# A scan and a top-2 mixture of adapters on one core: a new search in the tail, a rank for every operation, and A loaded in 512 B rows

## The chip, the core and the metric

The kernel runs on one core of a Trainium2 chip. The metric is the time of one execution in device microseconds (us). The core has five engines that work side by side: TensorE (PE in the profile, PEld for its weight loads), VectorE (DVE), ScalarE (ACT), GpSimd (POOL) and SyncE (SP), which here only issues transfers. Sixteen DMA engines move the data between the chip's memory (HBM) and the on-chip memory (SBUF). Matmul results land in eight banks of PSUM.

## The reference

First a linear recurrence over 6400 steps, in each of 8 batches and 128 channels; its 51,200 rows of 128 are then the tokens `x` of a mixture of 8 adapters of rank 16, of which each token uses the two with the largest logits.

```python
for t in range(S):                       # a, b: [8, 6400, 128] float32
    h = a[:, t] * h + b[:, t]
    out[:, t] = h
x = out.reshape(51200, 128)
logits = x @ w_gate                      # w_gate [128, 8]
topk = the two largest logits of each row
w = softmax over those two
delta[row] = sum over the two: w * ((x[row] @ A[e]) @ B[e])   # A [8,128,16], B [8,16,128]
return x + delta
```

## The kernel before

The tokens are cut into 100 chunks of 512 (`C`), a chunk into 4 blocks of 128 (`J`). What follows names the operations as the program does; a number behind the name is the chunk (`sc99`), the unit or the gate group.

**Loads.** `la` and `lb` bring two chunks of a and b at a time, 512 KB each, into one of 6 slots of `a_tm` and `b_tm` (`load`, L546, issued by SP). The first four chunks come singly. In most pairs ("paired" chunks) a row of SBUF takes 8 consecutive tokens, 4 KB; chunks 4 to 11 are "flat", with 2 KB per row. The constants come over ACT's queue (L471): A as `[d, e, r]`, pieces of 64 B, then w_gate, then B. `ch` (DVE, L489) casts all three to fp16 in `cst_h`.

**Front, by chunk.** PE transposes a and b into channel-major PSUM tiles pA and pB (`A`, `B`, or `P` for a mixed pair of halves; L567). ACT copies pA to `a_st` (`ae`, L585). DVE's scan `sc` (L618) reads `a_st` and pB and writes x in fp16, channel-major, to `xT` (24 slots); it starts from the last column of the scan before, so the scans follow one another in order.

**Logits, by unit.** A unit is 6 blocks (4 in the first three and the last four units, so that the last four units are chunks 96 to 99). `Z` (PE, L638) multiplies a block of x by `[A | w_gate]`, 136 columns, into pZ; `ze` (ACT, L644) copies the unit to `zl`.

**Gates, by group.** A group is 4 units; the first two groups have 1 and 2 units, the last five (17 to 21) have 2, 1, 1, 1 and 1. For each row of 8 logits the function `gating` finds the two largest and their weights: `g1` first maximum (DVE, L672), `2` logits minus it (L674), `3` -1e30 where that is at least 0 (L676), `5` added, which masks the maximum (L679), `g4` second maximum (DVE, L681), `6` minus it (L683), `7` the two differences added (L685), `w1` sigmoid (ACT, L687), `g8` times "is one of the two" (DVE, L693), which gives `g`. Operations 2, 3, 5, 6 and 7 run on GpSimd (then named `q2` to `q7`), but on DVE in the last six groups (`WIDE_DVE`, 16 to 21).

**Back, by chunk.** `mu` multiplies z by g into `zw` (GpSimd, L712; for the last ten chunks on DVE, as `md`, L716, by the list `MU_DVE`). `T` transposes zw on PE (L725); `te` copies the result to `zwT` (DVE, L734, for some chunks ACT, L731). `D` (PE) adds x, by a product with the identity (L739), and delta, zwT times B (L740), in pO; the last 12 chunks use the banks of pA and pB too. `oe` (ACT, L749) copies the block to `outt`, and SP stores two chunks at a time (L784, 512 KB), the last four chunks singly (256 KB).

One store goes out in parts: `SPLIT = {68: [93, 32, 3]}` cuts the store of chunks 68 and 69 by rows of SBUF into three transfers, of 93, 32 and 3 of its 128 rows.

**The order** on every engine is not written out by hand: `Program.schedule` plans it before the kernel is built. Every operation has a rank, and each engine's operations are sorted by it:

```python
rank[op.i] = op.base + (TEMPLATE[op.kind][op.k] ...) + NUDGE.get(op.name, 0.0)
```

`base` is the chunk's place, `TEMPLATE` an offset for each kind and place in a period of 6 chunks, and `NUDGE` an offset for single operations, nearly all of them in chunks 0 to 17 and from 78 on. Among the operations within `WINDOW[engine]` of the smallest rank the planner takes the one that can start first by its own cost estimates. `waits` then derives the semaphore waits.

Of the kernel before, what the change touches and what calls it, by code (L numbers as in the profile page):

```python
# [10 lines left out]
PERIOD = 6  # L11
# [7 lines left out]
Q_RATE = {3: 3.6e-3, 5: 2.1e-3, 7: 2.1e-3}  # L19
# [87 lines left out]
EARLY = -400  # L107
LEAD = [1, 2]
TAPER = [2, 1, 1, 1, 1]
WIDE_DVE = [1, 2, 3, 4, 5, 6]  # L110
TE_LAST = [1, 2, 4, 6, 8, 10]
TAIL_UNITS = [4, 4, 4, 4]
HEAD_UNITS = [4, 4, 4]
# [47 lines left out]
    "q7": [1.073],  # L161
    "q8": [35.473],
    "g7": [-1.33],
    "g8": [-0.424],
}


# [721 lines left out]
```

## Time and profile before

| | before |
|---|---|
| time, median of 3 runs (lowest to highest) | 203.87 us (203.84 to 204.08) |
| profiled execution, its own time | 204.1 us |
| its span in the profile | 202.2 us |
| mean granted clock of TensorE | 0.995 |
| bytes read from HBM, written | 52.56 MB, 26.21 MB |
| DMA packets under 512 B | 3702 of 30999 |

The span runs from the first to the last record of the profiled execution; the execution's own time also has what lies around it. A line of the form `L618 DVE TENSOR_TENSOR_SCAN xT<-a_st,xT,pB 128x512 ... x96` is a group of instructions: line of the kernel, engine, operation, what it writes and reads, its shape and how many there are. A row of the timeline begins with the start and the duration in us; in brackets stands how long the engine was idle before and what ended it. "issue" is time in which the engine waited for nothing that the profile shows. The busy time of a DVE row includes what of it overlaps its neighbours, so the step from one start to the next is the better price of a short instruction.

### The profile page before, as it was taken

How to read it: one execution, taken by the hardware profiler on the slowest of the kernel's cores; microseconds unless marked ns; L12 is line 12 of the kernel's file. 1: busy time of each engine (PE TensorE's matmuls, PEld its weight loads, DVE VectorE, ACT ScalarE, POOL GpSimd, SP SyncE). 2: the span in 40 equal slices, each digit the busy share in tenths (PEclk: the TensorE clock that was granted, in tenths of full speed). 3: DMA queues.
4: the chain of work that ended last, by engine and by line, in shares of the span. 5: the costliest groups of instructions: out<-in, count | busy, mean ns of one | idle time of the engine just before them, and what ended most of it. 6: DMA issues, size and time to landing. Idle time of an engine off the chain costs nothing.

```text
span 202.2 us, 7464 instructions
## 1 busy us (share of the span) xinstructions
PE 181.5 (90%) x3120; PEld 157.6 (78%) x3120; DVE 176.2 (87%) x291; ACT 172.7 (85%) x314; POOL 139.1 (69%) x176
## 2 busy tenths in 40 slices
PE   6978899999999999999999998987898997989971
PEld 6678777888888888888888887876787886877751
DVE  0679799999999999999999999986898997999970
ACT  2448799999998999999999998987797988978792
POOL 1016559998788898888888889796878997462000
PEclk9999999999999999999999999999999999999998
DMA  6999999999999999999999999999999999999984
GB/s 193 371 390 391 407 410 408 399 413 406 406 412 415 407 410 409 420 410 406 410 414 406 410 410 415 409 411 414 409 411 412 411 416 410 401 377 385 356 331 177
DMA packets 30999, 79.26 MB, mean 392 GB/s; under 512 B 3702, under 2 KB 3830, under 8 KB 30966
## 3 DMA queue, kind: packets, MB, share of 16 engines
q1 hardware_dynamic: 29494, 78.39, 98.6%
q10 hardware_dynamic: 1472, 0.40, 0.9%
q8 instruction: 25, 0.41, 0.8%
q14 instruction: 8, 0.07, 0.1%
HBM read 52.56 MB, written 26.21 MB: 390 GB/s over the span
## 4 chain that ended last, share of the span: by engine, by line
PE 35%; DVE 21%; DMA 14%; ACT 4%; issue 2%; POOL 1%; SPq 0%; DVEq 0%
DVE xT L618 11%; PE pA L567 7%; DMA b_tm<-in_b_dram 7%; PE pZ L638 7%; DMA a_tm<-in_a_dram 6%; PE pB L567 5%; PE pO L725 5%; PE pO L739 5%; PE pO L740 4%; DVE zwT L734 4%; DVE zw L716 3%; ACT outt L749 1%; ACT zl L644 1%; DVE g L693 1%; ACT a_st L585 1%
## 5 line engine op out<-in xcount | busy, mean ns | idle before, releaser
L618 DVE TENSOR_TENSOR_SCAN xT<-a_st,xT,pB 128x512 f16<-128x512 f32 x96 | 120.3, 1253 | 10.3 <-PE pB L567 6.3
L712 POOL TENSOR_TENSOR zw<-zl,g 128x512 f16<-128x512 f32 x90 | 94.3, 1064 | 16.8 <-DVE g L693 11.7
L567 PE MATMUL pA<-ident_f,a_tm 64*128 64x64 f32 (+1 forms) x752 | 68.4, 232 | 4.9 <-DMA b_tm<-in_b_dram 3.1
L567 PE MATMUL pB<-ident_f,b_tm 64*128 64x64 f32 (+1 forms) x752 | 68.7, 232 | 1.9 <-DMA a_tm<-in_a_dram 0.9
L585 ACT COPY a_st<-pA 128x512 f32<-128x512 f32 x100 | 59.8, 606 | 11.4 <-PE pA L567 6.6
L567 PEld LDWEIGHTS pA<-ident_f,a_tm 64*128 64x128 f32 (+1 forms) x752 | 55.5, 139 | 10.8 <-DMA b_tm<-in_b_dram 3.6
L567 PEld LDWEIGHTS pB<-ident_f,b_tm 64*128 64x128 f32 (+1 forms) x752 | 55.4, 139 | 6.9 <-DMA a_tm<-in_a_dram 1.2
L644 ACT COPY zl<-pZ 128x816 f32<-128x816 f32 (+1 forms) x69 | 57.6, 834 | 2.9 <-PE pZ L638 2.7
L749 ACT COPY outt<-pO 128x512 f32<-128x512 f32 x92 | 54.7, 606 | 3.3 <-PE pO L740 2.4
L739 PE MATMUL pO<-ident_h,xT 128*128 128x128 f16 x368 | 50.9, 221 | 2.1 <-ACT zwT L731 1.2
L740 PE MATMUL pO<-cst_h,zwT 128*128 128x128 f16 x368 | 50.1, 219 | 0.0
L739 PEld LDWEIGHTS pO<-ident_h,xT 128*128 128x128 f16 x368 | 40.6, 113 | 3.8 <-ACT zwT L731 1.7
L638 PE MATMUL pZ<-cst_h,xT 128*128 128x136 f16 x400 | 36.1, 225 | 3.4 <-DVE xT L618 2.3
L740 PEld LDWEIGHTS pO<-cst_h,zwT 128*128 128x128 f16 x368 | 36.5, 99 | 0.8 <-issue 0.8
L725 PE MATMUL pO<-ident_h,zw 128*128 128x128 f16 x368 | 35.1, 220 | 1.1 <-POOL k L685 0.4
L638 PEld LDWEIGHTS pZ<-cst_h,xT 128*128 128x128 f16 x400 | 26.4, 115 | 8.4 <-DVE xT L618 5.2
L734 DVE COPY zwT<-pO 128x512 f16<-128x512 f16 x76 | 30.7, 407 | 0.7 <-PE pO L725 0.6
L725 PEld LDWEIGHTS pO<-ident_h,zw 128*128 128x128 f16 x368 | 22.5, 97 | 4.8 <-issue 1.0
L674 POOL TENSOR_TENSOR k<-zl,m 128x192 f32<-128x192 f32 (+2 forms) x16 | 7.9, 493 | 14.1 <-DVE m L672 14.0
L683 POOL TENSOR_TENSOR L<-k,m 128x192 f32<-128x192 f32 (+2 forms) x16 | 7.8, 490 | 9.3 <-DVE m L681 9.3
L676 POOL TENSOR_SCALAR L<-k 128x192 f32<-128x192 f32 (+2 forms) x16 | 12.8, 801 | 1.4
L731 ACT COPY zwT<-pO 128x512 f16<-128x512 f16 x16 | 9.6, 597 | 3.3 <-PE pO L725 3.3
(43 smaller groups left out, 104.7 us busy)
## 6 DMA issues: line engine op xcount, KB each, us to landing
a_tm<-in_a_dram SPq DMA_DIRECT2D x48, 512.0 KB, 13.2
b_tm<-in_b_dram SPq DMA_DIRECT2D x48, 512.0 KB, 13.3
out_dram<-outt SPq DMA_DIRECT2D x47, 512.0 KB, 13.2
a_tm<-in_a_dram SPq DMA_DIRECT2D x4, 256.0 KB, 4.5
out_dram<-outt SPq DMA_DIRECT2D x4, 256.0 KB, 3.3
b_tm<-in_b_dram SPq DMA_DIRECT2D x3, 256.0 KB, 5.5
out_dram<-outt SPq DMA_DIRECT2D x1, 372.0 KB
b_tm<-in_b_dram ACTq DMA_DIRECT2D x1, 256.0 KB, 3.3
```

The lines of the kernel that those rows point to most:

```text
L567: last = eng["pe"].transpose(*args)
L585: lambda: eng["act"].copy(a_st[c % NA][:, :], pA[:, c % 2, :]), fr(c, "ae"))
L618: last = eng["dve"].tensor_tensor_scan(out=x[:, s0:s1], data0=a_st[c % NA][:, s0:s1], data1=pB[:, c % 2, s0:s1], initial=init, op0=ALU.mul ...
L638: last = eng["pe"].matmul(pZ[:, k // (n // 2), o : o + W], xblock(b0 + k), Awg_h)
L644: return eng["act"].copy(zl[:, zb : zb + n, :].rearrange("p (h k) w -> p h (k w)", h=2), pZ[:, :, 0 : n // 2 * W])
L676: lambda e: e.tensor_scalar(out=ll, in0=kk, scalar1=0.0, scalar2=-1.0e30, op0=ALU.is_ge, op1=ALU.mult), dve=not main)
L712: lambda: eng["pool"].tensor_tensor(out=wv, in0=zv, in1=gv, op=ALU.mult), ba(gi, c, "mu"))
L725: last = eng["pe"].transpose(ptile[:, k * 128 : k * 128 + 128], zw[w][:, k, :], ident_h[:, :])
L734: lambda: eng["dve"].tensor_copy(zwT[w][:, :], ptile[:, 0:C]), ba(gi, c, "te"))
L739: eng["pe"].matmul(dst, xblock(b0 + k), ident_h[:, :], start=True, stop=False)
L740: last = eng["pe"].matmul(dst, zwT[w][:, k * 128 : k * 128 + 128], B_h, start=False, stop=True)
L749: lambda: eng["act"].copy(outt[:, o0 : o0 + n, :].rearrange("p k w -> p (k w)"), bank),
```

## The change

It has five parts.

1. **A in 512 B rows.** A is loaded as `araw`, 128 rows of 512 B: row (e, h) holds 8 of the 128 channels (`l`) by 16 ranks (`r`) of expert e. As this is not the layout `cst_h` needs, it is rearranged on chip: two small reductions of the identity on DVE give `own` and `pick`, GpSimd multiplies `araw` by `own` (`cr`, 128x1024, into `spread`), PE sums 8 products with shifted views of `pick` into pZ (`cm`), and ACT copies the sum to `cst_h` (`cc`). Every `Z` depends on `cc` now. `ch` casts w_gate and B alone and is ranked earlier.

2. **A rank per operation.** `TEMPLATE` and `WINDOW` are all zero, and `NUDGE` names a rank for every operation, so that each engine runs its operations in the order of these ranks. The lists of who does what are by chunk now: `te` on ACT in 1, 7, 13, and so on each 6 up to 73, then 78, 80, 82, 83, 84, 89, 91, 92, 94, 96, 97 and 98 (before: the same up to 73, then 79, 85, 90, 92, 94, 96, 98 and 99); `mu` on DVE in 82, 84, 86 and 90 to 99 (before: 90 to 99).

3. **max8 in small groups.** In groups of at most 4 blocks (`TOP8`; groups 0 and 18 to 21) DVE's `max`, which gives the 8 largest of a row in order, runs once per block into `v8`. Operations 2 and 6 subtract its first and second column; 3, 5 and the second reduction fall away.

4. **Gates on GpSimd.** `GATE_DVE` names the gate operations that stay on DVE; all others of 2, 3, 5, 6 and 7 run on GpSimd, in the last groups too. In group 19 (chunk 97) this puts 2, 6 and 7 on GpSimd, in group 20 (chunk 98) 2 and 6, in group 21 (chunk 99) none.

5. **Two output copies on DVE, and the split.** `oe` of chunks 95 and 97 moves from ACT to DVE (`od`). The store of chunks 68 and 69 goes out as 124 and 4 rows.

Besides, one cost estimate for GpSimd's operation 3 and one for `w1` are other numbers, `paired` is renamed `woven`, and there is code for halved chunks and filler transposes that empty lists (`HALF`, `FILL`) leave out.

```diff
 NUDGE = {
-    "A0": -7.373, "A1": 6.112, "A10": -1.64, ...
+    "A0": 404.647, "A1": 403.572, "A10": 13.623, ...       # every operation has one
-WINDOW = {'pe': 42.345, 'act': 35.431, 'dve': 24.751, 'pool': 5.955, 'sp': 63.924}
+WINDOW = {'pe': 0.0, ...}
-WIDE_DVE = [1, 2, 3, 4, 5, 6]
-TE_LAST = [1, 2, 4, 6, 8, 10]
+GATE_DVE = ['2_14', '2_17', '2_18', '2_21', '3_14', '3_16', '5_17', '6_21',
+            '7_16', '7_17', '7_18', '7_20', '7_21']
-TE_ACT = [1]
-MU_DVE = [1, 2, 3, 4, 5, 6, 7, 8, 9, 10]
+TE_ACT = [1, 7, 13, 19, 25, 31, 37, 43, 49, 55, 61, 67, 73, 78, 80, 82, 83, 84, 89, 91, 92, 94, 96, 97, 98]
+MU_DVE = [82, 84, 86, 90, 91, 92, 93, 94, 95, 96, 97, 98, 99]
+OE_DVE = [95, 97]
-SPLIT = {68: [93, 32, 3]}
+SPLIT = {68: [124, 4]}
+TOP8 = 4
 ...
-            ("ca", 0.94, cst_f[:, 0:128].rearrange("p (e r) -> p e r", e=E),
-             moe_A.rearrange("e d r -> d e r")),
+            ("ca", 0.3, araw[:, :], moe_A.rearrange("e (h l) r -> (e h) (l r)", l=DL)),
 ...
+        o_cr = P.add(
+            "pool", "cr", 2.1, [(o_c[0], True), (o_own, True)],
+            lambda: eng["pool"].tensor_tensor(
+                out=spread[:, :, :].rearrange("q l (e r) -> q l e r", e=E),
+                in0=araw[:, :].rearrange("q (l r) -> q l r", l=DL).unsqueeze(2).broadcast_to([128, DL, E, R]),
+                in1=own[:, :].unsqueeze(1).unsqueeze(3).broadcast_to([128, DL, E, R]),
+                op=ALU.mult),
+            START,
+        )
+        def gather():
+            for k in range(DL):
+                last = eng["pe"].matmul(
+                    pZ[:, 0, 0:128], pick[:, DL - 1 - k : DL - 1 - k + 128], spread[:, k, :],
+                    start=k == 0, stop=k == DL - 1)
+            return last
+        o_cc = P.add("act", "cc", 0.3, [(o_cm, True)],
+                     lambda: eng["act"].copy(cst_h[:, 0:128], pZ[:, 0, 0:128]), (EARLY, "cc", 0))
 ...
+            top = nb <= TOP8
+            def maxes():
+                for k in range(nb):
+                    last = eng["dve"].max(out=t8[:, k, :], in_=Lp[:, k, :])
+                return last
+            if top:
+                b1, b2 = (t8[:, :, k : k + 1].to_broadcast([128, nb, E]) for k in (0, 1))
+                d2 = wide(2, ..., lambda e: e.tensor_tensor(out=kk, in0=Lp, in1=b1, op=ALU.subtract))
+                d5 = wide(6, ..., lambda e: e.tensor_tensor(out=ll, in0=Lp, in1=b2, op=ALU.subtract))
+            else:
+                d2, d5 = search()        # 2, 3, 5, g4, 6 as before
 ...
+            if c in OE_DVE:
+                o_oe[c] = P.add("dve", f"od{c}", ..., lambda: eng["dve"].tensor_copy(ov, bv), ...)
+            else:
+                o_oe[c] = P.add("act", f"oe{c}", ..., lambda: eng["act"].copy(ov, bv), ...)
```

More of the change, by code (lines that the diff above doesn't have):

```diff
@@ new lines @@
+    "la": [0.0, 0.0, 0.0],
+    "lb": [0.0, 0.0, 0.0],
+    "A": [0.0, 0.0, 0.0, 0.0, 0.0, 0.0],
+    "B": [0.0, 0.0, 0.0, 0.0, 0.0, 0.0],
+    "ae": [0.0, 0.0, 0.0, 0.0, 0.0, 0.0],
+    "sc": [0.0, 0.0, 0.0, 0.0, 0.0, 0.0],
+    "Z": [0.0, 0.0, 0.0, 0.0],
+    "ze": [0.0, 0.0, 0.0, 0.0],
+    "g1": [0.0],
+    "g2": [0.0],
+    "g3": [0.0],
+    "g4": [0.0],
+    "g5": [0.0],
+    "g6": [0.0],
+    "w1": [0.0],
+    "w2": [0.0],
+    "p1": [0.0],
+    "p2": [0.0],
+    "p3": [0.0],
+    "mu": [0.0, 0.0, 0.0, 0.0, 0.0, 0.0],
@@ new lines @@
+    "T": [0.0, 0.0, 0.0, 0.0, 0.0, 0.0],
+    "te": [0.0, 0.0, 0.0, 0.0, 0.0, 0.0],
+    "D": [0.0, 0.0, 0.0, 0.0, 0.0, 0.0],
+    "oe": [0.0, 0.0, 0.0, 0.0, 0.0, 0.0],
+    "st": [0.0, 0.0, 0.0],
+    "ta": [0.0, 0.0, 0.0, 0.0, 0.0, 0.0],
+    "md": [0.0, 0.0, 0.0, 0.0, 0.0, 0.0],
+    "wu": [0.0],
+    "fi": [0.0, 0.0, 0.0, 0.0, 0.0, 0.0],
+    "ch": [0.0],
+    "cm": [0.0],
+    "cc": [0.0],
+    "mb": [0.0],
+    "q2": [0.0],
+    "q3": [0.0],
+    "q5": [0.0],
+    "q6": [0.0],
+    "q7": [0.0],
@@ L588, in front @@
             r0 = rows[c]
-            if not paired(c):
+            o_fi = []
+            for k in range(FILL.get(c, 0)):
+                o_fi.append((P.add(
+                    "pe", f"fi{c}_{k}", 0.109, [(o_id, True)] + get(o_sc, c - 2),
+                    lambda: eng["pe"].transpose(pB[:, c % 2, 0:128], ident_f[:, :], ident_f[:, :]), fr(c, "fi")), True))
+            if not woven(c):
                 o_A[c] = P.add("pe", f"A{c}", 0.109 * J, deps_a(c), trans(part_a(c)), fr(c, "A"))
-                o_B[c] = P.add("pe", f"B{c}", 0.109 * J, deps_b(c), trans(part_b(c)), fr(c, "B"))
+                o_B[c] = P.add("pe", f"B{c}", 0.109 * J, deps_b(c) + o_fi, trans(part_b(c)), fr(c, "B"))
                 add_ae(c)
@@ L669, in wide @@
                              lambda: f(eng["pool"]), ga(gi, f"q{kind}"))
-            d1 = P.add("dve", f"g1_{gi}", 0.142 + nb * E * 1.04e-3, [(o_ze[u], True) for u in range(u0, u0 + n)] + old,
-                       lambda: eng["dve"].tensor_reduce(out=v1, in_=Lp, axis=X, op=ALU.max), ga(gi, "g1"))
-            d2 = wide(2, [(d1, True)] + old,
-                      lambda e: e.tensor_tensor(out=kk, in0=Lp, in1=bc(v1), op=ALU.subtract), dve=not main)
-            d3 = wide(3, [(d2, True)],
-                      lambda e: e.tensor_scalar(
-                          out=ll, in0=kk, scalar1=0.0, scalar2=-1.0e30, op0=ALU.is_ge, op1=ALU.mult), dve=not main)
@@ L686, in gating, with search @@
-            a1 = P.add("act", f"w1_{gi}", 0.15 + nb * E * 0.86e-3, [(d6, True)] + old,
+            top = nb <= TOP8
+            t8 = v8[s][:, 0:nb, :] if top else None
+            def search():
+                d2 = wide(2, [(d1, True)] + old,
+                          lambda e: e.tensor_tensor(out=kk, in0=Lp, in1=bc(v1), op=ALU.subtract))
+                d3 = wide(3, [(d2, True)],
+                          lambda e: e.tensor_scalar(
+                              out=ll, in0=kk, scalar1=0.0, scalar2=-1.0e30, op0=ALU.is_ge, op1=ALU.mult))
+                d3 = wide(5, [(d3, True)],
+                          lambda e: e.tensor_tensor(out=ll, in0=ll, in1=kk, op=ALU.add))
+                d4 = P.add("dve", f"g4_{gi}", 0.142 + nb * E * 1.04e-3, [(d3, True)],
+                           lambda: eng["dve"].tensor_reduce(out=v2, in_=ll, axis=X, op=ALU.max), ga(gi, "g4"))
+                d5 = wide(6, [(d4, True)],
+                          lambda e: e.tensor_tensor(out=ll, in0=kk, in1=bc(v2), op=ALU.subtract))
+                return d2, d5
@@ new lines, in maxes, with first @@
+            def maxes():
+                for k in range(nb):
+                    last = eng["dve"].max(out=t8[:, k, :], in_=Lp[:, k, :])
+                return last
+            def first():
+                return eng["dve"].tensor_reduce(out=v1, in_=Lp, axis=X, op=ALU.max)
+            d1 = P.add("dve", f"g1_{gi}", 0.09 + 0.075 * nb if top else 0.142 + nb * E * 1.04e-3,
+                       [(o_ze[u], True) for u in range(u0, u0 + n)] + old, maxes if top else first, ga(gi, "g1"))
+            if top:
+                b1, b2 = (t8[:, :, k : k + 1].to_broadcast([128, nb, E]) for k in (0, 1))
+                d2 = wide(2, [(d1, True)] + old,
+                          lambda e: e.tensor_tensor(out=kk, in0=Lp, in1=b1, op=ALU.subtract))
+                d5 = wide(6, [(d1, True)] + old,
+                          lambda e: e.tensor_tensor(out=ll, in0=Lp, in1=b2, op=ALU.subtract))
+            else:
+                d2, d5 = search()
@@ L687, in gating @@
+            d6 = wide(7, [(d2, True), (d5, True)],
+                      lambda e: e.tensor_tensor(out=kk, in0=kk, in1=ll, op=ALU.add))
+            a1 = P.add("act", f"w1_{gi}", 0.19 + nb * E * 0.86e-3, [(d6, True)] + old,
                        lambda: eng["act"].activation(sg, kk, ACTF.Sigmoid), ga(gi, "w1"))
@@ L693, in gating, with back_part @@
                            lambda e: e.scalar_tensor_tensor(
-                               out=gg, in0=ll, scalar=0.0, in1=sg, op0=ALU.is_ge, op1=ALU.mult), dve=True)
+                               out=gg, in0=ll, scalar=0.0, in1=sg, op0=ALU.is_ge, op1=ALU.mult))
         stored = [0]
         def back(gi, c):
+            if c in HALF:
+                back_part(gi, c, c, c * J, J // 2)
+                back_part(gi, c, NCH + HALF.index(c), c * J + J // 2, J // 2)
+            else:
+                back_part(gi, c, c, c * J, J)
+            while stored[0] < len(stores) and sum(stores[stored[0]]) <= c + 1:
+                if c in HALF:
+                    store_half(c, c, 0)
+                    store_half(c, NCH + HALF.index(c), J // 2)
+                else:
+                    store(*stores[stored[0]])
+                stored[0] += 1
+        def back_part(gi, ch, c, b0, n):
             u0 = groups[gi][0]
-            b0, n = c * J, J
             q0 = b0 - units[u0][0]
@@ L793, in store, with store_half @@
             for k in range(m * J):
+                olast[q + k] = op
+        def store_half(ch, c, j):
+            q = (ch * J + j) % NO
+            n = J // 2
+            r0 = rows[ch]
+            dst = out[r0 : r0 + C, :].rearrange("(p j) d -> p j d", j=J)[:, j : j + n, :]
+            op = P.add(
+                "sp", f"st{c}", n * 128 * D * 4 / LOAD_RATE, [(o_oe[c], True)],
+                lambda: eng["sp"].dma_start(dst, outt[:, q : q + n, :]), (PERIOD * (ch // PERIOD), "st", ch % PERIOD // 2),
+                sem=dma_sem(f"stx{c % 4}"),
+            )
+            o_st[c] = op
+            for k in range(n):
                 olast[q + k] = op
```

148 lines of the change are left out of this document (66 added, 82 removed), and 257 rows, old and new, of the table NUDGE.

## The prediction

> **What bounds the kernel now.** I read the page first: the span, the engines' shares, the row of the DMA engines.
>
> ```profile
> span 202.2 us, 7464 instructions
> PE 181.5 (90%) x3120; PEld 157.6 (78%) x3120; DVE 176.2 (87%) x291; ACT 172.7 (85%) x314; POOL 139.1 (69%) x176
> DMA  6999999999999999999999999999999999999984
> ```
>
> Four engines are near 90%, and the DMA engines are full from the second slice to the last but two. So I cut the span into stretches. The columns are the stretch, its length, then busy time and instruction count of PE, PE's weight loads, DVE, ACT and POOL, then PE's clock, the DMA share and GB/s.
>
> ```profile
> 4.00:6.00 2.00, 2.00 (x13) 1.93 (x12) 0.00 (x0) 0.31 (x3) 0.00 (x0) 1.00 1.05 263
> 6.00:8.00 2.00, 1.66 (x12) 0.95 (x9) 1.29 (x2) 1.12 (x3) 0.00 (x0) 1.00 1.06 391
> 60.00:80.00 20.00, 19.31 (x368) 17.22 (x367) 19.12 (x29) 18.90 (x36) 17.73 (x23) 1.00 1.03 410
> 140.00:160.00 20.00, 18.20 (x343) 15.94 (x340) 17.71 (x26) 17.55 (x32) 15.25 (x18) 1.00 1.04 411
> 180.00:185.00 5.00, 4.08 (x57) 3.21 (x56) 5.00 (x15) 3.62 (x8) 3.05 (x3) 1.00 1.03 388
> 185.00:190.00 5.00, 4.51 (x70) 3.85 (x69) 5.00 (x21) 4.60 (x10) 0.00 (x0) 1.00 0.92 346
> 192.00:193.00 1.00, 0.84 (x16) 0.67 (x13) 1.00 (x5) 1.00 (x4) 0.00 (x0) 1.00 0.96 365
> 193.00:194.00 1.00, 0.67 (x9) 0.33 (x7) 0.97 (x4) 0.94 (x3) 0.00 (x0) 1.00 0.38 141
> ```
>
> From 6 us to 185 us the DMA engines are full: this stretch is bound by them. PE and DVE are close behind at 60 to 80 (19.3 and 19.1 of 20), and by 140 to 160 they have idle time, because they wait for loads, as PE's timeline says in brackets (first row below). From 185 on the share falls while DVE has no idle time: there the DMA engines wait for stores that DVE's work holds back. So two things are worth time: bytes moved badly at the start, and DVE's work at the end. The second row below is a third, smaller thing: PE stood 0.72 us in the middle of a chunk with no wait that the profile knows.
>
> ```profile
> 143.77 0.27 PE L567 MATMUL pA<-ident_f,a_tm 64*128 64x64 f32 x1 [0.91 <-DMA b_tm<-in_b_dram]
> 169.04 0.22 PE L739 MATMUL pO<-ident_h,xT 128*128 128x128 f16 x1 [0.72 <-issue]
> ```
>
> The chain that ended last closes with chunks 99 and 96:
>
> ```profile
> 195.69 0.41 PE pB L725 x4
> 196.13 0.59 ACT zwT L731
> 196.77 0.25 PE pB L739
> 197.44 0.59 ACT outt L749
> 198.04 0.59 ACT outt L749
> ```
>
> Its last copy ends at 198.63. The last store is issued there, and a store takes at least 3.1 us to land:
>
> ```profile
> DMA to landing us min/median/max: 3.1/12.9/15.3
> ```
>
> That gives 201.7; the span ends 0.5 later. The profiled execution took 204.1 us, 1.9 above its span, and the median of the three runs is 203.87, 0.2 below it. I take a change of the span off the median.
>
> **The change, part by part. A in 512 B rows.** The stretch 4 to 6 us moves 263 GB/s where 6 to 8 moves 391, at the same share. The shortfall is 128 GB/s times 2 us, 256 KB, which at 391 GB/s is 0.65 us. The loads of the constants:
>
> ```profile
> cst_f<-in_moe_A_dram ACTq DMA_DIRECT2D x1, 64.0 KB, 5.0
> cst_f<-in_moe_B_dram ACTq DMA_DIRECT2D x1, 64.0 KB, 5.2
> ```
>
> A moves in 1024 pieces of 64 B, B's equal bytes in 128 rows of 512 B, and the stretch in which B lands (2.29 plus 5.2) shows no dip. So A in rows like B's returns most of 0.65; the gate's 32 B pieces stay. I take 0.5, between 0 (the loads are not what the end waits for) and 0.65. DMA share stays full to 185, so it is passed on to every load.
>
> What it adds: GpSimd multiplies 1024 elements a row, PE sums 8 matmuls, ACT copies, before the first logits.
>
> ```profile
> L712 POOL TENSOR_TENSOR zw<-zl,g 128x512 f16<-128x512 f32 x90 | 94.3, 1064 | 16.8 <-DVE g L693 11.7
> ```
>
> Two of these are 2.1 us. A is issued at 1.18 and lands 5.0 later, at 6.2 at the latest; product 8.3, matmuls 8.9. They stand in PE's queue ahead of chunk 2's transposes, which began at 7.21, so those start 0 to 1.7 us later, and ACT's copy stands ahead of a_st of chunk 2. What hides it is that loads are limited by the DMA engines, whose queue does not drain for it, and that DVE waits for loads later (17.71 of 20 at 140). Cost 0; 1.7 if that cover were gone. The two small reductions that DVE gains at the start lie before its first scan at 6.57.
>
> **The rank per operation.** On every engine the order is nearly the old one up to chunk 75: a reduction and a copy change places, two gate operations on GpSimd slip behind one multiplication. Cost 0. Later, the loads of b for chunks 82 and 84 and of a for 86 stand two transfers of 512 KB further back, 1.28 us each at 410 GB/s, so PE waits near 150. The loads of chunks 86 and 88 close at the same places in the queue as before, so the delay ends there. Cost 0 to 1.0 on the path; I take 0, since the place of the last load is the same and DVE's idle time lies in this stretch.
>
> **The tail on DVE.** Prices are steps from one start to the next where DVE is never idle:
>
> ```profile
> 181.61 1.26 DVE L618 TENSOR_TENSOR_SCAN xT<-a_st,xT,pB 128x512 f16<-128x512 f32 x1
> 182.79 0.15 DVE L672 TENSOR_REDUCE m<-zl 128x4 f32<-128x32 f32 x1
> ...
> 188.40 0.18 DVE L681 TENSOR_REDUCE m<-L 128x4 f32<-128x32 f32 x1
> 188.50 0.19 DVE L672 TENSOR_REDUCE m<-zl 128x4 f32<-128x32 f32 x1
> 188.60 0.41 DVE L734 COPY zwT<-pA 128x512 f16<-128x512 f16 x1
> 188.94 0.18 DVE L674 TENSOR_TENSOR k<-zl,m 128x32 f32<-128x32 f32 x1
> 189.03 0.68 DVE L716 TENSOR_TENSOR zw<-zl,g 128x512 f16<-128x512 f32 x1
> 189.64 0.17 DVE L676 TENSOR_SCALAR L<-k 128x32 f32<-128x32 f32 x1
> ...
> 194.94 1.29 DVE L716 TENSOR_TENSOR zw<-zl,g 128x512 f16<-128x512 f32 x2
> ```
>
> Scan 1.18, 32-wide gate operation 0.10, zwT copy 0.34, multiplication 0.61; I take 0.2 for a 96-wide one, between the 32-wide step and the copy. From the end of the last scan (182.79) to the last multiplication (196.23) DVE has before: 8 copies 2.7, 10 multiplications 6.1, 32 gate operations 3.2, three of 96 wide 0.6: 12.6, and 0.8 of small gaps. After: 6 copies 2.0, 10 multiplications 6.1, 12 max8 of 8 elements, 10 gate operations 1.0, two of 96 wide 0.4, one output copy. No row shows a max8. A 32-wide step less 24 elements at the scan's 2.3 ns is 0.045; if four do not overlap, each is a full 0.18. I take 0.10, the row it is nearest to: 1.2, from 0.5 to 2.2. Nor is there an output copy on DVE: between 0.34 (the 16-bit copy) and 1.18 (the scan, which also reads 32-bit PSUM); I take the multiplication's 0.61, also 512 elements of 32 bit. Sum 11.3, against 12.6: 1.3 less, from 0.1 to 2.3. Between the scans of chunks 92 and 99 DVE loses three copies (1.0) and 0.6 of gate work and gains three multiplications (1.8): 0.2 more. Net 1.1 earlier, and with A's 0.5 the last multiplication ends at 194.6 instead of 196.2.
>
> Behind it the chain is the old one: transposes, ACT copy, matmuls, ACT copy, 2.4 us. Chunk 99's zwT copy moves to DVE behind the last multiplication, chunk 97's output copy follows it; SP's store of 97 waits for that copy, and only the two last stores are queued behind it, whose data come later still. ACT loses two output copies and gains one zwT copy (8 for 7) there, no difference. Last copy 197.0, landing 200.1, span 200.6.
>
> **The floor of the DMA engines.** The last load is issued at 164.04:
>
> ```profile
> L546 SPq DMA_DIRECT2D b_tm<-in_b_dram x1: 577/577/577, 164.0 to 164.0; - x1
> DMA to landing us min/median/max: 12.9/12.9/12.9
> ```
>
> It lands at 176.9. Behind it stand 16 stores of 524 KB and 4 of 262 KB, 9.44 MB, in both kernels. At the 388 GB/s of 180 to 185 they take 24.3 us: 201.2, and with 0.5 for the end 201.7. So the present end, 202.2, is only 0.5 above this floor. A's 0.5 lowers it to 201.2. DVE's 200.6 lies under it: the DMA engines bind again, and of DVE's 1.1 us half is worth nothing.
>
> **The split.** One store of 128 rows, 512 KB, goes out as 124 and 4 instead of 93, 32 and 3. SP has an issue less, 0.4 us, hidden since SP is 12 us ahead. I take 0; its other end is the last rival.
>
> Sum: 202.2 to 201.1, 1.1 less; 204.1 becomes 203.0, and the median 202.8. If PE's 0.72 us stall falls elsewhere, the floor hides it.
>
> **Rivals.** *Only A counts.* If waits between engines eat DVE's 1.1 us, the end moves by A's 0.5 alone: 203.4. For: the gaps of 0.8 in the present tail. Against: the tail has fewer steps that follow each other.
>
> *GpSimd's gates come late.* For chunks 97 and 98 DVE's max8 is followed by three and two operations on GpSimd, then ACT or DVE, then g. Rows for 32 wide:
>
> ```profile
> 13.66 0.24 POOL L674 TENSOR_TENSOR k<-zl,m 128x32 f32<-128x32 f32 x1 [12.18 <-DVE m L672]
> 13.98 0.33 POOL L676 TENSOR_SCALAR L<-k 128x32 f32<-128x32 f32 x1
> ```
>
> Three are 0.8 to 1.0 us, and DVE has 1.3 queued meanwhile: just covered. But if each also waits for a multiplication on DVE (0.61), five lose 3.0, of which perhaps 2 show: the last multiplication at 196.6, span 202.6, 204.2. GpSimd has no instruction after 185 in this trace, so nothing here speaks for or against. The Trainium skill, GPSIMD Engine Reference, Specifications, says that GpSimd shares its SBUF interfaces with VectorE, and that instructions of VectorE with two SBUF inputs contend; no run here shows it yet.
>
> *The split loads a quarter of the DMA engines* (slower). At 193 to 194 the share is 0.38 while stores are still landing: some DMA engines are out of work, others behind. If 124 rows lie on four of the 16, each moves 127 KB; at 388/16 = 24 GB/s that is 5.2 us, against 1.35 for an even share, 3.9 more. The three that held 93 rows had the same 5.1 before; the fourth is new. If it is not ahead of the others, what it can soak up is its idle time from 185 to 194, (1.03 - 0.92) x 5 + 0.07 + 0.65 = 1.3; with A's 0.5 the end is 2.1 later, 206.0; if it is ahead by over 2.6, nothing is lost; it is slower from a lead of under 2.1. I take 205.2, a middle. The Trainium skill, DMA: Bandwidth & Descriptors, section Why a DMA increments its semaphore by 16 and not by 1, says that a DMA of SP runs on the largest number of engines up to 16 that divides its slowest dimension, the lowest-numbered ones: 4 for 124 rows and 3 for 93. By that rule the forecast stands only if the fourth engine was ahead; the trace names no engine.
>
> **How the numbers follow.** Forecast 202.8: 0.55. Only A, 203.4: 0.12. GpSimd late, 204.2: 0.13. Split, 205.2: 0.20. The range 202.0 to 205.0 takes in the forecast's ends (max8 at 0.045 and A's 0.65 to one side), the first two rivals and the better half of the last. Within 0.2%, about what a measurement of this kernel can tell from no change, is 203.46 to 204.28. Faster: 0.50 of the forecast's 0.55, 0.08 of "only A", 0.05 of the split's good leads: 0.63. Same: 0.15, mostly GpSimd late. Slower: 0.22.
>
> **What would show it.** Right: the stretch 4 to 6 us near 390 GB/s; the last load landing near 176.4; DVE's last multiplication near 194.6 and max8 steps near 0.10; no dip of the DMA share at 193. GpSimd late: idle DVE before its g rows after 185. Split: share near 0.25 late, with a last landing far behind the last copy. Wrong altogether: the last load landing later than 176.9, or a last multiplication after 196.

## The result and the profile after

| | before | after |
|---|---|---|
| median, 20 runs each (lowest to highest) | 203.94 us (203.75 to 204.23) | 203.22 us (202.69 to 204.12) |
| ratio, 95% interval | | 0.9967 (0.9957 to 0.9978) |
| profiled execution, its span | 204.1, 202.2 us | 202.69, 200.7 us |

The change is worth 0.7 us, 0.33%; forecast were 1.1 us and 202.8, in a range that holds the measured time. The scatter has grown: the profile after is of the fastest of its 20 runs, half a microsecond under their median.

The page after, its span and the slices of the DMA engines, and the row of the small packets:

```profile
span 200.7 us, 7490 instructions
PE 180.8 (90%) x3128; PEld 157.9 (79%) x3128; DVE 176.5 (88%) x287; ACT 172.7 (86%) x317; POOL 140.5 (70%) x182
DMA  5999999999999999999999999999999999999995
DMA packets 30089, 79.26 MB, mean 395 GB/s; under 512 B 2664, under 2 KB 2920, under 8 KB 30056
```

The same stretches as before (length, then busy time and count of PE, its loads, DVE, ACT, POOL, then the clock, the DMA share and GB/s):

```profile
4.00:6.00 2.00, 2.00 (x10) 1.70 (x9) 0.00 (x0) 0.13 (x1) 0.62 (x1) 1.00 1.07 362
6.00:8.00 2.00, 2.00 (x20) 1.77 (x19) 1.07 (x1) 1.17 (x2) 1.31 (x1) 1.00 1.06 398
180.00:185.00 5.00, 4.20 (x63) 3.50 (x61) 4.77 (x16) 4.47 (x10) 2.86 (x5) 1.00 0.98 374
185.00:190.00 5.00, 4.59 (x76) 4.07 (x73) 4.83 (x23) 5.00 (x12) 0.96 (x5) 1.00 0.93 354
193.00:194.00 1.00, 0.83 (x15) 0.69 (x12) 1.00 (x2) 0.27 (x2) 0.00 (x0) 1.00 1.02 381
196.00:198.00 2.00, 0.00 (x0) 0.00 (x0) 0.00 (x0) 0.59 (x1) 0.00 (x0) 0.94 0.64 244
```

The shortfall at 4 to 6 us has shrunk from 128 to 36 GB/s; A's 1024 packets of 64 B are gone. DVE's tail after the last scan:

```profile
181.31 1.27 DVE L787 TENSOR_TENSOR_SCAN xT<-a_st,xT,pB 128x512 f16<-128x512 f32 x1
...
185.82 0.36 DVE L858 MAX8 v<-zl 128x8 f32<-128x8 f32 x4
186.11 0.40 DVE L938 COPY zwT<-pA 128x512 f16<-128x512 f16 x1
...
189.03 0.63 DVE L858 MAX8 v<-zl 128x8 f32<-128x8 f32 x8
189.60 0.42 DVE L938 COPY zwT<-pB 128x512 f16<-128x512 f16 x1
...
192.10 0.68 DVE L955 COPY outt<-pO 128x512 f32<-128x512 f32 x1
192.70 0.18 DVE L883 SCALAR_TENSOR_TENSOR g<-L,sd 128x32 f32<-128x32 f32 x1
192.92 1.29 DVE L920 TENSOR_TENSOR zw<-zl,g 128x512 f16<-128x512 f32 x2
194.21 0.42 DVE L938 COPY zwT<-pB 128x512 f16<-128x512 f16 x1
194.55 0.68 DVE L955 COPY outt<-pA 128x512 f32<-128x512 f32 x1
```

A max8 steps 0.07 us (0.29 for four, 0.57 for eight), an output copy on DVE 0.60. The last multiplication ends at 194.21, 2.0 earlier than before. ACT's last copy then ends at 196.61, the same 2.4 behind it:

```profile
196.02 0.59 ACT L958 COPY outt<-pA 128x512 f32<-128x512 f32 x1
```

What follows is seen best in the 16 completions of each transfer, one for each DMA engine, as the trace records them on the transfer's semaphore (a transfer has landed when the last of them is in). For the last store, in us:

```
kernel        issue starts  ends    the completions, in order
before        198.65        199.36  15 from 200.86 to 201.04; 201.73
after         197.28        197.84  12 from 199.43 to 199.61; 200.12 200.14 200.21 200.22
```

The first engines are done 1.5 to 1.6 us after SP's issue has ended, the slowest 0.8 to 0.9 us after them, and the span ends 0.5 after that. So the end has three terms: when the last copy ends, how long SP takes to issue the last store, and how far the slowest DMA engine is behind. The same records show where that last term comes from. In the kernel before, the 16 completions of b's eighth load lay within 0.63 us (18.23 to 18.86), those of the last load within 5.62 (171.30 to 176.92). The page's queue of instructions has 25 packets of 16 KB:

```profile
q8 instruction: 25, 0.41, 0.8%
```

Each begins some 255 PE instructions after the one before and lies on one DMA engine for about 1 us. The first begins at 18.81, and a's eighth load, which lands next, has its completions within 1.85 us instead of 0.63: one engine is set back. So it goes on. In the first profile of the changed kernel, the time behind the fastest engine, added up over the 16, was 2.4 us at 10 us and 44.8 at the last load. From one load to the next it rose by 0.7 us or more 25 times, and 23 of these rises lie from 0.5 us before to 2.5 us after the start of one of the 22 packets of that time; 36 of the 42 us came about there. So engines that get several packets fall behind, and at the end, where the share falls, they can catch up. Which engine a packet lies on, the trace doesn't name.

### The profile page after: what moved, and what is told of

Its sections match the earlier page's. It is cut to its first block, busy times and chain, and to the rows that moved or that the text cites. A ratio compares the mean times of both kernels' runs of the same rounds, so it can differ in the third digit from the quotient of the medians.

```text
span 200.7 us, 7490 instructions
## 1 busy us (share of the span) xinstructions
PE 180.8 (90%) x3128; PEld 157.9 (79%) x3128; DVE 176.5 (88%) x287; ACT 172.7 (86%) x317; POOL 140.5 (70%) x182
## 4 chain that ended last, share of the span: by engine, by line
PE 21%; DVE 18%; DMA 13%; POOL 7%; ACT 3%; issue 2%; SPq 0%; DVEq 0%
DVE xT L787 9%; DMA b_tm<-in_b_dram 7%; DMA a_tm<-in_a_dram 6%; PE pZ L807 4%; POOL zw L916 4%; PE pA L731 4%; PE pB L731 3%; PE pO L929 3%; DVE zw L920 3%; PE pO L943 3%; PE pO L944 3%; DVE zwT L938 2%; ACT zl L813 1%; POOL L L846 1%; DVE g L883 1%
## 5 line engine op out<-in xcount | busy, mean ns | idle before, releaser
L916 POOL TENSOR_TENSOR zw<-zl,g 128x512 f16<-128x512 f32 x87 | 92.0, 1068 | 21.9 <-DVE g L883 18.8
L938 DVE COPY zwT<-pO 128x512 f16<-128x512 f16 x72 | 29.2, 408 | 2.4 <-PE pO L929 2.0
L846 POOL TENSOR_SCALAR L<-k 128x192 f32<-128x192 f32 (+2 forms) x15 | 12.2, 810 | 3.2 <-DVE k L844 2.0
L935 ACT COPY zwT<-pO 128x512 f16<-128x512 f16 x20 | 11.9, 603 | 1.3 <-PE pO L929 1.0
L787 DVE TENSOR_TENSOR_SCAN xT<-a_st,pB 128x512 f16<-128x512 f32 (+1 forms) x8 | 7.5, 937 | 4.9 <-ACT a_st L749 4.7
L853 POOL TENSOR_TENSOR L<-k,m 128x192 f32<-128x192 f32 (+2 forms) x17 | 8.5, 500 | 2.5 <-DVE m L851 2.4
```

What stands on the lines that cost most here:

```text
L787: last = eng["dve"].tensor_tensor_scan(out=x[:, s0:s1], data0=a_st[c % NA][:, s0:s1], data1=pB[:, c % 2, s0:s1], initial=init, op0=ALU.mul ...
L846: lambda e: e.tensor_scalar(out=ll, in0=kk, scalar1=0.0, scalar2=-1.0e30, op0=ALU.is_ge, op1=ALU.mult))
L916: lambda: eng["pool"].tensor_tensor(out=wv, in0=zv, in1=gv, op=ALU.mult), ba(gi, c, "mu"))
L938: lambda: eng["dve"].tensor_copy(zt, ptile[:, 0 : n * 128]), ba(gi, c, "te"))
```

## The experiments

The kernels ran in four rounds, each round with the kernel before beside them on one chip; its medians were 203.77 to 203.89. The table has the medians, with the 95% interval of the ratio to the kernel before.

| kernel | runs | median us | ratio (interval) |
|---|---|---|---|
| x_again | 12 | 203.34 | 0.9980 (0.9965 to 0.9994) |
| x_old_a | 12 | 203.40 | 0.9980 (0.9968 to 0.9992) |
| x_split93 | 12 | 203.51 | 0.9984 (0.9972 to 0.9996) |
| x_nosplit | 12 | 203.90 | 1.0002 (0.9992 to 1.0012) |
| x_split119 | 6 | 205.56 | 1.0082 (1.0069 to 1.0096) |
| x_split92 | 8 | 202.98 | 0.9962 (0.9948 to 0.9976) |
| x_oe_act | 6 | 203.20 | 0.9970 (0.9959 to 0.9981) |
| x_gates_dve | 11 | 203.52 | 0.9988 (0.9978 to 0.9998) |
| x_old_search | 4 | 206.23 | 1.0122 (1.0109 to 1.0135) |
| x_before_max8 | 11 | 203.93 | 1.0001 (0.9992 to 1.0010) |
| x_warm8 | 12 | 203.58 | 0.9982 (0.9969 to 0.9995) |
| x_best1 | 5 | 203.00 | 0.9960 (0.9946 to 0.9974) |

**The changed kernel again.**

> The changed kernel once more, to be compared with the three runs beside it on the same chip, and for a second profile of it. Every theory: a median near 203.2 us, 0.7 below the kernel before. The first profile was of the fastest of its 20 runs (202.69), so I expect this profile to show an end some 0.5 us later. Theory L (the end is the issue of the last store, plus 2.2 us, plus what the slowest of the 16 DMA engines is behind the others): the last store is issued near 197.3 again, and the later end shows as a larger spread among the 16 completions of the last store, 1.3 us instead of 0.8. Theory C (the chain of computation itself comes later in slower runs): the last store is issued at 197.8, with the spread unchanged.

This profile is of an execution of 204.37 us, the slowest of its 12 runs and 1.7 longer than the first one. The last stores' issue and landing, the first profile's and then this one's:

```profile
L989 SPq DMA_DIRECT2D out_dram<-outt x2: 564/821/1078, 196.2 to 197.3; - x2
DMA to landing us min/median/max: 2.9/3.2/3.4
```

```profile
L989 SPq DMA_DIRECT2D out_dram<-outt x2: 1103/1106/1108, 196.4 to 197.5; - x2
DMA to landing us min/median/max: 4.4/4.6/4.9
```

Its last multiplication ends at 194.44, 0.23 later; the last store is issued 0.25 later but lands 1.7 later. Of its 16 completions 15 lie from 200.14 to 200.35 and one at 201.90. So it is mostly theory L: of the 1.7 us, 0.25 come from the later issue, 1.0 from the slowest engine (1.76 behind the first, instead of 0.80), and the other 0.5 from something that theory L had as a constant, since the issue itself took 1.11 us instead of 0.56. The slowest engine shows already in the store after the split one, where 15 engines are within 6.1 us and the last 2.1 behind them. By a jump of that size it is one that carries the 124 rows, and, unlike the receivers in the first profile (4.6 to 5.9 us ahead of the slowest), it was ahead by only some 2.5.

**The split.** Four sizes:

```diff
-SPLIT = {68: [124, 4]}
+SPLIT = {68: [93, 32, 3]}      # x_split93
+SPLIT = {}                     # x_nosplit
+SPLIT = {68: [119, 9]}         # x_split119
+SPLIT = {68: [92, 32, 4]}      # x_split92
```

> The changed kernel with the store of chunks 68 and 69 cut into 93, 32 and 3 rows as before. Prediction's step (124 and 4 costs nothing against 93, 32 and 3): the same within 0.2 us. Theory L with receivers that are ahead: the engines that take the large part get 33 rows either way, one engine fewer is loaded, and all others carry 2 rows more (0.3 us); the end moves by -0.2 to +0.3. The prediction's last rival (a fourth engine that is not ahead): this kernel faster by 1 us or more.

> The changed kernel with the store of chunks 68 and 69 in one transfer, even over the engines. Theory L: the engines that are 5 to 6 us ahead keep that lead, the slowest ones carry 1.3 us more than with the split; the bulk of the last store's completions stays near 199.5 and the slowest end 0.4 to 1.2 later: 203.6 to 204.4 us. Rival (the split is worth nothing, since the store queue drains before the end): the same within 0.2 us. Rival of the prediction (the split loads four engines that are not ahead): 1 us faster or more.

> The changed kernel with the store of chunks 68 and 69 cut into 119 and 9 rows. In the profile after, just before that store, 7 of the 16 DMA engines are 4.6 us or more ahead of the slowest and the other 9 are within 3.2; with 124 and 4 rows four of the leading ones were loaded with 5 us, two of which then became the slowest. If 119 rows lie on 7 engines (17 rows, 2.8 us each) and these are the 7 that lead, the last store's 16 completions lie within 0.5 us of each other and the time is 0.3 to 0.6 below the changed kernel's 203.3. Rival (the engines 5 to 7 are not among the leaders): one of them is the slowest, the spread is over 1.5 and the time 203.6 or more. Rival (the split spreads over all engines whatever the rows): as without a split, 203.9.

> The changed kernel with the store of chunks 68 and 69 cut into 92, 32 and 4 rows. Where 124 and 4 gave four DMA engines 32 rows each (5.3 us at 24 GB/s) and the others none, this gives the four 26 rows (4.3 us) and each of the others 2 (0.3 us). Theory L: the receivers that became the slowest (by 0.7 us in the first profile after, by 1.6 in the second) come 1.0 earlier, the others 0.3 later; the last store's completions lie within 0.8 us and the time is 0.2 to 0.5 below the changed kernel's, 202.8 to 203.1, with a smaller scatter from run to run. Rival (the slowest engines at the end are not the receivers, but those behind for another reason): the same or up to 0.3 slower.

How many engines each part lies on can be counted: the stores that share the split one's semaphore leave 74 records on it with 124 and 4, 82 with 119 and 9, 88 with 93, 32 and 3, and 90 with 92, 32 and 4. Four whole stores are 64 of them; the rest are 10, 18, 24 and 26, which is 4+4, 7+9, 3+16+3 and 4+16+4, and 2 each time. The Trainium skill, DMA: Bandwidth & Descriptors, section Why a DMA increments its semaphore by 16 and not by 1, has the rule for it: the largest number up to 16 that divides the rows, and what is missing to 16 written at once, which makes one record more for each part on fewer engines. The records agree to the last one.

The last store:

```
kernel       issue starts  ends    the completions, in order
x_nosplit    196.65        197.41  11 from 198.91 to 199.08; 199.50 199.52 199.58; 200.38; 201.41
x_split119   197.61        198.69  13 from 200.19 to 200.36; 200.89 201.00; 203.15
x_split92    197.01        197.76  14 from 199.26 to 199.44; 200.47 200.51
```

Without a split one engine ends 2.3 us behind the bulk, and the whole gain of the change is lost (the kernel before has a split too), although the last copy ends at 196.6 as in the first profile. That one engine is read in the windows too, as a share of 0.06, one sixteenth, from 200 to 201:

```profile
199.00:200.00 1.00, 0.00 (x0) 0.00 (x0) 0.00 (x0) 0.00 (x0) 0.00 (x0) 0.55 0.16 59
200.00:201.00 1.00, 0.00 (x0) 0.00 (x0) 0.00 (x0) 0.00 (x0) 0.00 (x0) 0.50 0.06 25
```

119 rows lay on 7 engines, and it seems that one of these was not far enough ahead: one engine ends 2.8 us behind the bulk, and the median is 2.2 up. The expectation that the 7 leading engines are these 7 fell; its first rival held. 93, 32 and 3 differ from 124 and 4 by less than the runs can tell. 92, 32 and 4, which takes 1 us from the four receivers and gives 0.3 to all others, has the lowest median of all, as expected; its interval still overlaps that of the changed kernel. The sign of the theory behind it did not show: the 16 completions lie within 1.24 us and not 0.8, and the runs still scatter from 202.59 to 203.80.

**A.** The old load and cast, without `own`, `pick`, `cr`, `cm` and `cc`:

```diff
-            ("ca", 0.3, araw[:, :], moe_A.rearrange("e (h l) r -> (e h) (l r)", l=DL)),
+            ("ca", 0.94, cst_f[:, 0:128].rearrange("p (e r) -> p e r", e=E), moe_A.rearrange("e d r -> d e r")),
```

> The changed kernel with A loaded in 64 B pieces as before, without the rearrangement on chip; all else as changed. In the first profiles the mean completion of b's eighth load was 18.08 us after against 18.52 before, and that of the last load 173.83 against 174.23, so A's rows gave the DMA engines 0.4 us. Prediction's step (the gain is passed on to the end): 0.4 to 0.5 slower than the changed kernel, 203.65, with the last load's mean completion 0.4 later. Rival (the end hangs on DVE's tail and on the slowest engine, which hide it): no slower than by 0.15, although the loads come 0.4 later.

The mean completion of the last load is 174.40, against 173.83 and 173.95 in the two profiles of the changed kernel: 0.5 later, and the last multiplication ends at 194.70, 0.3 to 0.5 later. Over all 14 profiles the gain is 0.4: the mean completion lies between 173.83 and 174.19 in the eleven with A in 512 B rows, and between 174.23 and 174.40 in the three with the old load. The last of the 16 completions scatters more, from 176.50 to 177.28 (mean 176.87) and from 176.92 to 177.40 (mean 177.21). The medians of the execution times differ by 0.06, which these runs can't tell from nothing, nor from 0.3. So the gain is real at the loads; what is left of it at the end, these runs don't show.

**The tail.** In these kernels the order is a list written out, that of the changed kernel (of the kernel before, in the last one) with only the named operations moved; their line numbers are higher for it. Six gate operations back on DVE; the two output copies back on ACT:

```diff
+GATE_DVE: '6_18', '2_19', '6_19', '7_19', '2_20', '6_20' added       # x_gates_dve
-OE_DVE = [95, 97]
+OE_DVE = []                                                         # x_oe_act
```

> The changed kernel with max8, but with operations 2, 6 and 7 of groups 18 to 21 all on DVE: six 32-wide operations more there, right behind the max8 of their group or one operation later; the order is otherwise kept. Prediction's step: 0.10 each, the last multiplication ends 0.6 later (194.8 instead of 194.2), and the end follows: 203.8 to 203.9. Rival (gates on GpSimd come late and DVE waits for them, as the prediction's second rival has it): the same or faster, by up to 0.3, since DVE's idle time of 0.2 us from 185 to 190 goes too. Rival L: under half of the 0.6 reaches the end, because the slowest DMA engine sets it.

> The changed kernel with the output copies of chunks 95 and 97 on ACT as before; every other operation keeps its place in the order. In the profile after, the copy on DVE steps 0.60 us (192.10 to 192.70) and stands once ahead of the last two multiplications, so these end 0.6 earlier, at 193.6. Prediction's step (DVE's tail sets the end, and ACT has room): 0 to 0.6 faster than the changed kernel's 203.3. Rival (ACT, busy for 5.00 of 5 us from 185 to 190, is late next): the two copies of 0.6 stand ahead of the last copies on ACT, the last copy ends 0.5 to 1.2 later than 196.6, and the time is 203.6 to 204.3. Rival L (the slowest DMA engine sets the end): within 0.2 either way.

With the gates on DVE the last multiplication ends at 194.85, 0.4 to 0.6 later as expected. The median is 0.2 to 0.3 higher, about half of the 0.6 expected or less; but the intervals overlap, so that a loss is likely and not shown. With the copies on ACT it ends at 193.98, 0.2 earlier and not 0.6, DVE's last copy then waits for PE, and ACT's last copy ends at 196.97, 0.36 later than in the first profile:

```profile
192.69 1.29 DVE L1015 TENSOR_TENSOR zw<-zl,g 128x512 f16<-128x512 f32 x2
194.75 0.42 DVE L1033 COPY zwT<-pB 128x512 f16<-128x512 f16 x1 [0.77 <-PE pB L1024]
```

The median is the changed kernel's, within 0.2 as rival L has it. The output copies on DVE are worth nothing that shows.

Then max8 itself, from both sides: taken out of the changed kernel's groups 18 to 21, and put alone into the kernel before, with all else in its old place.

```diff
-            top = nb <= TOP8                     # x_old_search; 2, 3, 5, 6 and 7 of these groups on DVE
+            top = nb <= TOP8 and gi < 18
+            top = gi >= 18                       # x_before_max8, in the kernel before
```

> The changed kernel with the old search in groups 18 to 21 (first maximum, operations 2, 3 and 5, second maximum, 6 and 7, all on DVE), spread over the places in the order that the changed kernel has; max8 stays in group 0. DVE gets 28 operations of 0.10 us for 16 max8 (0.07 each in the profile after) and 6 operations: 2.8 against 1.75, 1.05 us more, of which 0.2 before the last scan. Prediction's step: the last multiplication ends 1.0 later, near 195.2, and the time is 204.2 to 204.3. Rival L: less than half of it arrives at the end, 203.5 to 203.8.

> The kernel before, with max8 in groups 18 to 21 and nothing else: each group's first maximum becomes four max8, operations 3, 5 and the second maximum fall away, 2 and 6 subtract the first and second column; they stay on DVE, and all other operations keep the place that they have in the kernel before. After the last scan DVE loses 16 operations of 0.10 us and gains 16 max8, which step 0.07 in the profile after: 1.6 against 1.15. Prediction's step (DVE's tail sets the end): the last multiplication ends 0.45 earlier (195.8 instead of 196.2), up to 0.9 if waits from one dependent operation to the next go too, and the time falls with it, to 203.0 to 203.45. Rival L (the slowest DMA engine, or SP's issue, takes part of it): less than half arrives, 203.6 or more. Rival (the order, not the search, holds the last multiplication): it ends within 0.2 of 196.2.

The prediction's step misses in both. Put alone into the kernel before, max8 gains nothing: the last multiplication ends at 196.36 instead of 196.23, within 0.2, as the last rival has it. The multiplication before the last two and DVE's last gate rows, before and then with max8:

```profile
192.75 0.69 DVE L716 TENSOR_TENSOR zw<-zl,g 128x512 f16<-128x512 f32 x1
...
194.23 0.19 DVE L685 TENSOR_TENSOR k<-k,L 128x32 f32<-128x32 f32 x1
194.72 0.19 DVE L693 SCALAR_TENSOR_TENSOR g<-L,sd 128x32 f32<-128x32 f32 x1 [0.29 <-ACT sd L687]
```

```profile
192.91 0.69 DVE L831 TENSOR_TENSOR zw<-zl,g 128x512 f16<-128x512 f32 x1
...
194.07 0.19 DVE L800 TENSOR_TENSOR k<-k,L 128x32 f32<-128x32 f32 x1
194.84 0.19 DVE L808 SCALAR_TENSOR_TENSOR g<-L,sd 128x32 f32<-128x32 f32 x1 [0.58 <-ACT sd L802]
```

DVE is done with operation 7 0.16 us sooner and waits longer, for the last sigmoid, which stands in ACT's queue behind a zwT copy. ACT before, with max8 alone, and after:

```profile
193.93 0.59 ACT L731 COPY zwT<-pB 128x512 f16<-128x512 f16 x1
194.46 0.23 ACT L687 ACTIVATE sd<-k 128x32 f32<-128x32 f32 x1
```

```profile
194.09 0.59 ACT L846 COPY zwT<-pB 128x512 f16<-128x512 f16 x1
194.58 0.23 ACT L802 ACTIVATE sd<-k 128x32 f32<-128x32 f32 x1
```

```profile
191.71 0.26 ACT L877 ACTIVATE sd<-k 128x32 f32<-128x32 f32 x1
191.87 0.59 ACT L935 COPY zwT<-pA 128x512 f16<-128x512 f16 x1
192.67 0.59 ACT L935 COPY zwT<-pB 128x512 f16<-128x512 f16 x1 [0.22 <-PE pB L929]
```

With max8 alone that copy starts 0.16 later than before, because the multiplication that its data come from (the first row of each pair above) does: the last group's four max8, which take 0.28 us, stand ahead of it, where the old first maximum took 0.09. And before, there was little to gain behind it: operation 7 ended at 194.42, and the copy let the sigmoid start at about 194.41 (where the input was ready well before, sigmoids started 0.47 to 0.49 after the start of such a copy). So the chain runs from DVE over PE and ACT back to DVE. In the new order the sigmoid comes ahead of both copies, 2.75 us earlier. The other way round, the old search in the new order ends the last multiplication at 198.13, 3.9 later and not 1.0. Some rows of it:

```profile
184.34 0.18 DVE L938 TENSOR_TENSOR k<-zl,m 128x32 f32<-128x32 f32 x1
184.56 0.18 DVE L940 TENSOR_SCALAR L<-k 128x32 f32<-128x32 f32 x1
...
192.00 0.29 DVE L938 TENSOR_TENSOR k<-zl,m 128x32 f32<-128x32 f32 x2
192.97 0.42 DVE L1032 COPY zwT<-pB 128x512 f16<-128x512 f16 x1 [0.68 <-PE pB L1023]
```

A 32-wide operation that reads what the one right before it wrote starts 0.22 after it, not 0.10, and DVE's four waits for PE sum to 1.95 us (0.40, 0.53, 0.34 and 0.68). The order in which I put the added operations is mine, so 3.9 is what the old search costs at these places, not the least that it could cost.

**Two more.** Eight warm-up transposes fewer, to move the last instruction packet; and a kernel of what had helped.

```diff
-WARM0 = 12
-WARM = 16
+WARM0 = 8
+WARM = 8                          # x_warm8
+SPLIT = {68: [92, 32, 4]}         # x_best1: this, the 8 warm-ups, and the store of chunk 96 from ACT
+eng["act" if c == 96 else "sp"].dma_start(...)
```

> The changed kernel with 8 warm-up transposes on TensorE at the start instead of 16 (they feed nothing). In every trace so far TensorE's instructions are read in 25 packets of 16 KB, one for about 255 instructions, each on one of the 16 DMA engines and 0.9 to 1.5 us long; in the profile after, the last began at 195.91, at TensorE's instruction 6371 of 6372, while the last stores were on their way. 16 instructions fewer should put this packet behind the last matmul. Theory F (this packet is part of what the slowest engine is behind at the end): 24 packets before the last store lands, or a 25th too late to matter, and 0.1 to 0.5 faster than the changed kernel. Rival (the other slow engines, those with the large part of the split, are as late): the same within 0.2. Rival (the warm-up counts: the clock or the first transposes come late): slower by 0.3 or more, with the first scan later than 6.6.

> The changed kernel with the split in 92, 32 and 4 rows, 8 warm-up transposes, and the very last store (chunk 96) issued by ACT, right behind its own copy, instead of SP. In the profile after, that copy ended at 196.61 and SP issued the store at 197.28, because its issue before took 1.08 us; the first of the 16 completions came 2.15 after the issue. Theory: the issue comes 0.6 earlier, and with the slowest engine within 0.3 of the others the last landing is at 199.0 to 199.3: 201.7 to 202.2 us, 0.9% to 1.1% below the kernel before. Rival (the DMA engines, not the issue, set the end): no better than the two changes alone, 202.8 to 203.1.

The packet did not go: 25 again, the last at 195.44, at instruction 6342 of 6356. So theory F was not put to the test, and the median is no better; the first scan began at 6.84, against 6.93, so that the warm-up doesn't count by the sign named for it. In x_best1 the last store was issued at 196.57, right behind the copy, 0.7 earlier than in the first profile, and its first 13 completions lie from 198.89 to 199.07; but one engine ends at 200.36, and the median is that of x_split92. The issue was not what held the end any more; the slowest engine was. x_split92 and x_best1 are the best versions run, 0.9 us (0.4%) below the kernel before.

## Why the prediction was right, and where its steps were not

The change made the kernel faster, and the tail came sooner, as forecast. That the number is near is in part luck: the floor of the DMA engines, which set the forecast, is not what the runs show, and in the chain behind DVE's tail two errors offset each other.

- **A in 512 B rows**: right at the loads (0.40 at the mean of the last load, against 0.5 taken; 263 to 362 GB/s). The sign that was named for it, a last load landing near 176.4, did not show in the first profile: it landed at 176.89 against 176.92, with the slowest engine 5.86 us behind the fastest instead of 5.62. Over all profiles the last landing is 0.3 earlier, within a scatter of 0.8; so "it is passed on to every load" holds in the mean, and what a single execution has of it is up to the slowest engine.
- **The tail on DVE**: the terms were near. Max8 0.07 (0.10 taken), the copy 0.60 (0.61), a 96-wide operation 0.17 (0.2): 10.9 where I had 11.3; with 0.3 from the earlier last scan the last multiplication ended at 194.2 (194.6). In the new order the sum holds, with gaps of 0.8 as before (182.49 to 194.21). But the argument for it failed: that less work on DVE is enough. The wait of 0.29 for ACT's sigmoid, which I counted among "small gaps", was the last step of a chain that runs over PE and ACT; less work on DVE alone only lengthened it (0.58). Max8 without the new order gained nothing, and I had priced the order at 0; what the order is worth without max8 stays open.
- **Behind the last multiplication**: 2.4 us, as taken. Then SP issued the last store 0.67 after the copy, since its issue before took 1.08 us; "SP's store of 97 waits" was named in the prediction, and priced at 0. So of the 2.0 us by which the last copy ends sooner, 1.4 are left at the start of the last issue. The span by this chain, 200.6, is near the 200.7 of the first profile only by luck: the copy ended 0.4 sooner than forecast, the issue came 0.67 later, and the landing took 2.94 instead of 3.1; and this was the fastest run.
- **The floor of the DMA engines**: wrong as a mechanism. 200.7 lies under the "floor" of 201.2. The engines as a mean were not full at the end (share 0.64 from 196 to 198 us in the first profile); the last landing is that of one engine among 16, and how far it is behind differs from run to run. The run of 203.22 us has a span of 201.2, the floor's very number; as the runs under it show, that is luck. How the 0.4 us between forecast and result divide is not shown: between the two profiles of the changed kernel, 1.7 us apart, 1.0 were the slowest engine's, 0.5 those of SP's issue and 0.25 those of the chain.
- **The split**: 0 against 93, 32 and 3 was right within what the runs tell. The rival's mechanism, an engine under the large part that is not far enough ahead, showed in one profile, where by the size of the jump it made 1.0 of the 1.7 us of the run of 204.37. That the split is worth 0.5 us at all was not in the prediction.
- **GpSimd's gates come late**: not so. DVE stood 0.17 us in 185 to 190, that for PE, and with the same gates on DVE the last multiplication ends 0.4 to 0.6 later.
- **The rank per operation up to chunk 99's scan**: not tried by itself; the last scan began 0.30 earlier, no more than A explains (with the old load of A it began at 181.80, against 181.31 and 181.53).

## What to carry to other kernels

When an engine is never idle, look for the short wait just before its last step: it may end a chain that runs over other engines' queues, and then less work alone only lengthens it. Where the DMA engines are full, read a transfer's landing engine by engine: the end waits for the slowest of 16, and a gain in their mean can be hidden there. A transfer whose rows lie on a few engines can level them, but only if they are ahead.

## What the runs showed of the hardware that I had not expected

The instruction packets of TensorE, 16 KB for about 255 instructions, take a DMA engine 0.9 to 1.7 us each, and leave the 16 engines 5 to 6 us apart after 165 us of full load. The Trainium skill, Runtime: NRT & Kernel Launch, section Instruction fetch mechanics, tells of refills in blocks of 16 KiB, 256 instructions, and calls their cost mostly hidden; the blocks are those of this trace, but beside full DMA engines the cost is not hidden. From 186 us on, SP's issue of a store took 0.33 to 0.37 us in most cases (0.4 to 4.1 earlier, while the DMA engines were full), but 0.85 and 1.08 to 1.10 for two of the last ones in both profiles of the changed kernel, against 0.34 and 0.33 for the same two without a split and 0.35 and 0.33 with 92, 32 and 4. Why, no run shows. A 32-wide DVE operation starts 0.22 us after one of its kind whose result it reads, and 0.10 after one whose result it doesn't: the old search is a chain of seven operations of which each reads one before, with max8 it is one of three.
